# A retention and SwiGLU kernel on one core: the loads of the first four pairs, VectorE copies for the first pair, and sums and loads moved at the second token tile

## The chip, the core and the metric

The kernel runs on one core of a Trainium2 chip. The time is device microseconds of one launch. In these pages PE is TensorE (matmuls; PEld is its weight load), DVE is VectorE, ACT is ScalarE, POOL is GpSimd and SP is SyncE, which here only starts transfers. Each engine takes its own instructions in order and waits, where it must, for another engine or for a transfer (DMA). ACT and POOL can start transfers too. In such a queue a transfer is asked for when the engine arrives at the instruction.

## What is computed

```python
# q, k, v: (batch 8, heads 8, seq 576, head_dim 64), fp32
scores = scale * q @ k.T                       # scale = 1/sqrt(64)
gamma  = 1 - 2 ** (-5 - arange(heads))
rel    = pos[:, None] - pos[None, :]
D      = where(rel >= 0, gamma ** rel, 0)      # per head
att    = (scores * D) @ v
x      = att.transpose(0, 2, 1, 3).reshape(4608, 512)
g      = x @ w_gate                            # w_gate, w_val: (512, 1536)
y      = (g * sigmoid(g)) * (x @ w_val) @ w_out    # w_out: (1536, 512)
```

## The kernel before

**Attention.** The 64 heads are taken in 32 pairs `i`, four (`HP`) to a batch, a pair filling the 128 partitions. Retention is computed in chunks with a running state. `load(i)` (from L258) starts the transfers of a pair: the query and key in the layout for transposing (`qk`), the key (`kn`), the value (`v`) and the last rows of the value (`vl`, one transfer a head). `tick(t)` (L573) is one step of a pipeline three pairs deep. On PE it issues the own-chunk values of pair t-2, the state products of t-1, the earlier-chunk values of t-2 and the scores of t-1. What the other engines do for it stands in a list of pieces: first a copy of the even states (`even`) of t-1 together with the scaling of `kn` of pair t (`keys`), then the outputs of t-2 (`to_x`), the masks of t-1 (`own`, `states`), and the transposes of pair t into `qT` and `kT`, at last a load to come. `go_on(k)` (L595) issues the next k pieces, and the steps of the second half call it between their own instructions: once in an up step, three times in a down step, four times in `down0`.

For the first four pairs PE transposes query and key into three PSUM banks and ACT copies them out (L417, L420); from pair 4 on DVE transposes 32x32 blocks. `keys` run on ACT (L438), for pairs 10 to 12 on DVE (L435, by `vector(i)`). For pairs 12 to 19 (`light(i)`) ACT copies the outputs, and for the others DVE scales them.

**Weights.** They arrive as 64-bit numbers. `load_w(m)` (L343) starts the transfer of one block (1 MB) on ACT's queue, `split(j)` (L361) takes half a block apart on ACT, `rounding(j)` (L376) puts the fp32 value together on DVE. `load_w(0)`, `(1)` and `(2)` are called by `keys` of pairs 0, 1 and 2; every later one by the split that frees the place it goes to.

**The feed-forward part.** Its first token tile has 512 tokens and is done plainly: `up0(f)` (matmul L612) and `down0(f)` (L622) over 12 blocks of 128 hidden columns. The other four tiles have 1024 tokens each and go by a table of fast matrix multiplication (`UP`, `DOWN`): 26 up steps (L842) for each third (`qd`) of the hidden columns, and then 26 down steps (L881), each a product of a sum of input blocks with a sum of weight blocks. The sums of `w_out` (`out_sums`, POOL) are formed at the end of the first tile and stored in DRAM (`dn_ops`), on SP's queue, or on ACT's where a group is `late`. The sums of `w_gate` and `w_val` (`first_sums`, `w_sums`, issued by L648 through `add` and by L812) are formed in the up steps of the second tile on POOL, DVE and ACT, and stored (`up_ops`). Later tiles, and the down steps of the second one, fetch both through a ring of eight places (L739, SP), eight operands ahead.

Steps write into one of four PSUM banks. DVE reads a bank (L783, L786), ACT applies SiLU (L857), and DVE or POOL multiplies (L860, L864) into `hid`.

**Order.** The order on PE, DVE, ACT, POOL and SP is the order of the source from L906 on: ticks 0 to 5 with the first splits and roundings (from L908), then a list `plan` for `up0`, then the loop over `down0`, then the loop over the four large tiles (from L974). What stands before L906, such as the calls `load(0)` to `load(3)`, the identity matrix and the masks `near`, is put in order by the compiler's planner. Pairs 6 and on are loaded two pairs ahead by `next_load` (12 and 13 by `load` in the second tile's first up steps); the load of pair 10 is called in the plan's last but one block, that of pair 11 after the first `down0`. In the second tile (`n == 1`) ticks 12 to 17 lie in its up steps and 18 to 21 in its down steps, spaced out evenly by `merge` (L900): the latter come before down steps 0, 6, 13 and 19.

`first_sums(0)` is called in the `down0` loop, and `first_sums(qd + 1)` in up step 22 of the first two thirds of the second tile: four sums for the next third's first step (one each by ACT and DVE, two by POOL), then those of its second step, all ahead of that step's own bank reads in the queues.

Of the kernel before, what the change touches and what calls it, by code (L numbers as in the profile page):

```python
# [154 lines left out]
def kernel(  # L155
# [32 lines left out]
    nc = tc.nc  # L188
# [69 lines left out]
    def load(i):  # L258
# [6 lines left out]

        queues = (nc.sync, nc.scalar if i < 2 else nc.sync)

# [23 lines left out]
        for dst, src in ((kn, k), (t, v)):  # L291
            for hl in range(2):
                chunks(dst, src, hl)
        for hl in range(2):
            queues[hl].dma_start(out=last[half[hl]], in_=v[b, 2 * p + hl, CW:S, :])
        loaded[i] = (qk, kn, t, last)
# [10 lines left out]
    nc.sync.dma_start(out=tab[:, NCOL:], in_=decays[:, NCOL:])  # L307
    load(2)
    load(3)
    ident = const.tile([P, P], F32, name="ident")  # L310
# [9 lines left out]
    for hl in range(2):  # L320
        nc.gpsimd.affine_select(out=near[half[hl]], in_=inv[half[hl]].unsqueeze(2).to_broadcast([L, H, L]),
                                compare_op=ALU.is_ge, fill=0.0, base=0, pattern=[[0, H], [1, L]], channel_multiplier=-1)
        nc.gpsimd.tensor_copy(out=last_near[half[hl]], in_=near[half[hl], hl::2])


# [76 lines left out]
    def vector(i):  # L402

        return 10 <= i <= needed(1) - 2

    def transposes(i):
        p = i % HP
        qk, kn, vt, last = loaded.pop(i)
        qT = qp.tile([P, S], F32, tag="qT", name="qT")
        st[i] = dict(qT=qT, kn=kn, v=vt, last=last)  # L410
        pieces = []
        if i < HP:

            for t, src, bank in ((qT, qk[0], bankA), (kT, kn, bankB)):
                for c in range(NFULL):
                    nc.tensor.transpose(bank[:, ts(c, P)], src[:, c].rearrange("p h d -> p (h d)"), ident)
                nc.scalar.copy(out=t[:, 0:CW], in_=bank)  # L417
            nc.tensor.transpose(bankC[:, 0:P], qk[1].rearrange("p h d -> p (h d)"), ident)
            for n, t in enumerate((qT, kT)):
                nc.scalar.copy(out=t[:, CW:S], in_=bankC[:, n * L : (n + 1) * L])  # L420
        else:
            if light(i):
                def scale_q():

                    src = qk[:, 0].rearrange("p (j r) d -> p r j d", r=2)
                    for r in range(2):
                        nc.scalar.activation(out=src[:, r], in_=src[:, r], func=AF.Copy, scale=piece[:, 2 * p + r : 2 * p + r + 1])
                pieces.append(scale_q)
            for n, t in enumerate((qT, kT)):
                pieces.append(lambda n=n, t=t: nc.vector.transpose(out=t, in_=qk[:, n].rearrange("p j d -> p (j d)")))  # L430

        def keys():
            for hl in range(2):
                if vector(i):
                    nc.vector.tensor_scalar(out=kn[:, :, hl, :], in0=kn[:, :, hl, :],  # L435
                                            scalar1=key[:, 2 * p + hl : 2 * p + hl + 1], scalar2=None, op0=ALU.mult)
                else:
                    nc.scalar.activation(out=kn[:, :, hl, :], in_=kn[:, :, hl, :], func=AF.Copy,  # L438
                                         scale=key[:, 2 * p + hl : 2 * p + hl + 1])
            if i < RAWS:  # L440
                load_w(i)

        if light(i):
            return [lambda: (keys(), pieces[0]())] + pieces[1:]
        return [keys] + pieces
# [127 lines left out]
    def tick(t, lo=HP, hi=NP, spread=False, then=None):  # L573
# [10 lines left out]
        keys, *new = transposes(t) if lo <= t < hi else (lambda: None,)  # L584
        pieces.append(lambda: (copies(), keys()))
        if lo <= t - 2 < hi:
            pieces.extend(to_x(t - 2))
        pieces.extend(masks)
# [226 lines left out]

    def first_sums(qd):

        engines = [nc.scalar, nc.gpsimd, nc.vector, nc.gpsimd]
        for op, eng in zip(up[0][5], engines, strict=True):
            if op[0] == "neg":  # L820
                nc.scalar.mul(out=up_view(qd)(int(op[1])), in_=up_view(qd)(int(op[2])), mul=-1.0)
            else:
                add(eng, op, up_view(qd))
        w_sums(qd, 1)

    def up_step(n, qd, i):
# [17 lines left out]
        if busy:  # L844
            nc.scalar.dma_start(out=up_ops[qd][i].rearrange("p (g x) -> p g x", g=2), in_=w)
            if i == 22 and qd + 1 < NQ:
                first_sums(qd + 1)
            if qd + 1 == NQ and i >= 22:
# [90 lines left out]
    for f in range(2, NF):  # L939
# [4 lines left out]
        if f in tick_at:  # L944
            plan.append(lambda t=tick_at[f]: tick(t, HP, FIRST))
        if f == NF - 2:
            plan.append(lambda t=tick_at[f]: next_load(t))
# [10 lines left out]
    for m, f in enumerate(down_order):  # L958
        down0(f)
        if m == 0:  # L960
            next_load(9)
        go_on(4)
# [3 lines left out]
        if m == 8:  # L966
            first_sums(0)
        if m > 8:
# [12 lines left out]
    for n in range(1, NTILE):  # L981
# [3 lines left out]
        if n == 1:  # L985

            for i in range(N):
                ups.pop(0)()
                if i in (6, 14):
                    load(FIRST + i // 14)  # L990
        for a, b, steps in ((done, cut, ups), (cut, upto, [lambda i=i: down_step(n, i) for i in range(N)])):
            merge((0.0, ticks(a, b)), (0.5, steps))
        done = upto
# [30 lines left out]
```

## Time and profile before

| | |
|---|---|
| median of 6 runs | 1082.82 us (1080.19 to 1087.33) |
| the profiled execution | 1082.78 us, of which the span 1081.1 us |
| mean granted clock of TensorE | 0.991 |
| PE busy | 1041.9 us (96%) |
| DVE busy | 645.4 us (60%) |
| POOL busy | 401.7 us (37%) |
| ACT busy | 275.8 us (26%) |
| weight loads of PE (beside its matmuls) | 857.4 us (79%) |
| DMA, mean rate | 184 GB/s |

The profile cuts the span into 40 equal slices and gives each engine a digit for each slice, its busy share in tenths; PEclk is the clock that the throttle granted to TensorE in tenths of full speed. A group of instructions is shown as line, engine, operation, output and inputs with their shapes and the number of instructions, then its busy time and the mean of one in ns (or start and length in us where single instructions are listed), and in brackets the engine's idle time just before and what ended it. SPq is SP's queue, ACTq ScalarE's. A sum of busy times says little of the end: PE has 96% of the span, so what matters is where PE stands still and what ends each pause.

### The profile page before, as it was taken

The page shows a single profiled execution, that of the slowest core. Times are in us where ns is not written, and L with a number is a line of the kernel's source. Part 1 is how long each engine was busy: PE and PEld are TensorE (multiplying, and loading weights), DVE is VectorE, ACT ScalarE, POOL GpSimd, SP SyncE. Part 2 cuts the span into 40 slices and gives each one's busy share as a digit, 9 for nine tenths or more (in the row PEclk, how much of TensorE's full clock was granted, in tenths as well). Part 3 has the DMA queues.
Part 4 walks back from the last instruction along what each step waited for, and adds up shares of the span by engine and source line. Part 5 has one row for each costly group of instructions (what it writes and reads, how often), then busy time and mean ns, then how long its engine had stood idle before and what let it go on. Part 6 is the DMA issues. An engine that isn't in the chain of part 4 may idle for free.

```text
span 1081.1 us, 21477 instructions
## 1 busy us (share of the span) xinstructions
PE 1041.9 (96%) x8420; PEld 857.4 (79%) x8420; DVE 645.4 (60%) x1063; ACT 275.8 (26%) x588; POOL 401.7 (37%) x357
## 2 busy tenths in 40 slices
PE   5999995999999899999999999999999999999998
PEld 4545553688878788888888888888888888888887
DVE  1577743876877866754646868535267465244644
ACT  3465500223343211223232111122221012231110
POOL 1002369475455402741215025622151375122505
PEclk9899997999999999999999999999999999999999
DMA  9979766665567788767567778554565555555653
GB/s 226 236 227 250 212 177 197 190 193 173 167 177 197 234 192 246 207 178 199 147 171 213 180 188 248 155 150 137 154 174 152 161 177 154 152 151 158 182 167 98
DMA packets 304212, 198.58 MB, mean 184 GB/s; under 512 B 219632, under 2 KB 247280, under 8 KB 304112
## 3 DMA queue, kind: packets, MB, share of 16 engines
q1 hardware_dynamic: 272512, 152.80, 53.5%
q10 hardware_dynamic: 31600, 44.41, 12.2%
q8 instruction: 67, 1.10, 0.4%
q14 instruction: 33, 0.27, 0.1%
HBM read 157.04 MB, written 40.11 MB: 182 GB/s over the span
## 4 chain that ended last, share of the span: by engine, by line
PE 84%; DVE 6%; POOL 3%; issue 2%; DMA 2%; SPq 2%; ACT 1%; ACTq 0%; DVEq 0%; POOLq 0%
PE bankE L842 11%; PE bankA L842 11%; PE bankC L842 11%; PE bankB L842 11%; PE bankE L881 6%; PE bankB L881 6%; PE bankC L881 6%; PE bankA L881 6%; PE outer L482 2%; PE bankA L612 2%; PE bankC L612 2%; PE bankB L612 2%; DVE rest L783 2%; PE bankE L612 2%; PE outer L459 2%
## 5 line engine op out<-in xcount | busy, mean ns | idle before, releaser
L783 POOL TENSOR_TENSOR rest<-rest 128x512 f32<-128x512 f32 x56 | 79.1, 1418 | 297.4 <-DVE rest L783 279.0
L857 ACT ACTIVATE io<-rest 128x256 f32<-128x256 f32 x180 | 75.0, 417 | 347.1 <-DVE rest L783 301.3
L842 PE MATMUL bankC<-rest,arena 128*128 128x256 f32 x544 | 129.3, 381 | 1.5 <-DVE rest L783 1.4
L842 PE MATMUL bankA<-rest,arena 128*128 128x256 f32 x544 | 129.0, 380 | 1.3 <-DVE rest L783 1.3
L648 POOL TENSOR_TENSOR arena<-arena 128x512 f32<-128x512 f32 (+1 forms) x72 | 114.7, 1606 | 34.9 <-DMA up<-arena 25.2
L648 POOL TENSOR_TENSOR rest<-rest 128x256 f32<-128x256 f32 (+1 forms) x86 | 79.5, 944 | 126.0 <-DVE rest L384 88.9
L842 PE MATMUL bankB<-rest,arena 128*128 128x256 f32 x512 | 121.5, 380 | 1.2 <-DVE arena L860 0.8
L842 PE MATMUL bankE<-rest,arena 128*128 128x256 f32 x512 | 121.5, 380 | 0.2 <-DVE rest L783 0.2
L842 PEld LDWEIGHTS bankA<-rest,arena 128*128 128x128 f32 x544 | 103.1, 190 | 16.7 <-issue 2.1
L842 PEld LDWEIGHTS bankC<-rest,arena 128*128 128x128 f32 x544 | 102.8, 190 | 16.7 <-issue 2.6
L864 POOL TENSOR_TENSOR arena<-rest,io 128x256 f32<-128x256 f32 x72 | 51.9, 727 | 167.1 <-ACT io L857 167.1
L842 PEld LDWEIGHTS bankB<-rest,arena 128*128 128x128 f32 x512 | 97.0, 190 | 15.3 <-DVE arena L860 1.2
L842 PEld LDWEIGHTS bankE<-rest,arena 128*128 128x128 f32 x512 | 97.0, 190 | 13.9 <-issue 0.6
L783 DVE TENSOR_TENSOR rest<-bankB,rest 128x512 f32<-128x512 f32 x72 | 48.9, 687 | 64.7 <-PE bankB L842 46.7
L783 DVE TENSOR_TENSOR rest<-bankC,rest 128x512 f32<-128x512 f32 x72 | 49.0, 688 | 64.0 <-PE bankC L842 43.9
L783 DVE TENSOR_TENSOR rest<-bankE,rest 128x512 f32<-128x512 f32 x72 | 48.8, 686 | 63.7 <-PE bankE L842 45.5
L783 DVE TENSOR_TENSOR rest<-bankA,rest 128x512 f32<-128x512 f32 x72 | 48.8, 686 | 63.0 <-PE bankA L842 45.7
L860 DVE SCALAR_TENSOR_TENSOR arena<-rest,io 128x256 f32<-128x256 f32 x84 | 55.6, 666 | 12.3 <-ACT io L857 12.3
L881 PE MATMUL bankB<-arena 128*128 128x256 f32 x252 | 58.3, 381 | 0.0
L881 PE MATMUL bankA<-arena 128*128 128x256 f32 x252 | 58.1, 381 | 0.0
L881 PE MATMUL bankC<-arena 128*128 128x256 f32 x252 | 58.0, 380 | 0.0
L881 PE MATMUL bankE<-arena 128*128 128x256 f32 x252 | 57.9, 380 | 0.0
(155 smaller groups left out, 1627.2 us busy)
## 6 DMA issues: line engine op xcount, KB each, us to landing
arena<-up SPq DMA_DIRECT2D x234, 256.0 KB, 2.6
arena<-dn SPq DMA_DIRECT2D x104, 384.0 KB, 3.5
up<-arena ACTq DMA_DIRECT2D x78, 256.0 KB, 2.7
out_dram<-rest SPq DMA_DIRECT2D x32, 256.0 KB, 3.5
qk<-in_q_dram SPq DMA_DIRECT2D x112, 72.0 KB, 2.9
qk<-in_k_dram SPq DMA_DIRECT2D x112, 72.0 KB, 2.6
v<-in_v_dram SPq DMA_DIRECT2D x62, 128.0 KB, 2.9
kn<-in_k_dram SPq DMA_DIRECT2D x58, 128.0 KB, 3.0
```

Source lines behind the costliest of these rows:

```text
L459: m = nc.tensor.matmul(xo[half[hl ^ r * exchange(i)], c, r], s["v"][half[r], c, hl, :], ret[half[r], hl, c], start=(c == 0), stop=(c == 0) ...
L482: nc.tensor.matmul(xr[half[hl]] if c + 1 == NC else xo[half[hl ^ c % 2 * exchange(i)], c // 2, c % 2], state[half[hl], c, :], s["qT"][half ...
L612: nc.tensor.matmul(bank, w_up[:, f // 4, gv, f % 4, c // 2, (c % 2) * P : (c % 2 + 1) * P], xs[0][:, c, :], start=(c == 0), stop=(c == HP ...
L648: eng.tensor_tensor(out=dst, in0=srcs[0], in1=srcs[1], op=ALU.add if op[0] == "add" else ALU.subtract)
L783: eng.tensor_tensor(out=at(op[1]), in0=at(op[2]), in1=at(op[3]), op=ALU.add if op[0] == "add" else ALU.subtract)
L842: nc.tensor.matmul(b[:, gv * TB : (gv + 1) * TB], w[:, gv, ts(c, P)], rhs[:, c, :], start=(opens and gv == 0 and c == 0), stop=(c == 1), s ...
L857: nc.scalar.activation(out=s, in_=src[:, 0:TB], func=AF.Silu, scale=-1.0 if negative else 1.0)
L860: return lambda: nc.vector.scalar_tensor_tensor(out=dst, in0=src[:, TB : 2 * TB], scalar=-1.0, in1=s, op0=ALU.mult, op1=ALU.mult)
L864: nc.gpsimd.tensor_tensor(out=dst, in0=src[:, TB : 2 * TB], in1=s, op=ALU.mult)
L881: nc.tensor.matmul(b[:, m * TB : (m + 1) * TB], lhs[:, qd, ts(m, P)], w[:, qd], start=(opens and qd == 0 and m == 0), stop=(qd == NQ - 1), ...
```

## The change

Seven edits, of which the first three concern the start:

1. In `load`, the second head's transfers of pairs 2 and 3 are issued by POOL; before, by SP. `load(2)` and `load(3)` stand behind the identity matrix and the masks in the source.
2. The last rows of the value are one transfer for both heads from pair 4 on; before, two.
3. Pair 0's copies out of PSUM and its key scaling are on DVE; before, on ACT. `load_w(0)`, `(1)` and `(2)` are called by `keys` of pairs 1, 2 and 3.
4. In a tick whose outputs ACT copies (pairs 12 to 19), the outputs ride with the first piece; before, they were a piece of their own. Every later piece of such a tick is issued one `go_on` earlier.
5. `first_sums` of thirds 1 and 2 is issued in two parts: two sums at up step 22, the other two and the second step's sums at step 25.
6. The load of pair 11 is called in the plan, ahead of the last block's `out_sums` groups; before, after the first `down0`.
7. In the second tile, ticks 18 to 21 come before down steps 2, 7, 13 and 19.

```diff
@@ load
-        queues = (nc.sync, nc.scalar if i < 2 else nc.sync)
+        queues = (nc.sync, nc.scalar if i < 2 else nc.gpsimd if i < HP else nc.sync)
...
-        for hl in range(2):
-            queues[hl].dma_start(out=last[half[hl]], in_=v[b, 2 * p + hl, CW:S, :])
+        if i < HP:
+            for hl in range(2):
+                queues[hl].dma_start(out=last[half[hl]], in_=v[b, 2 * p + hl, CW:S, :])
+        else:
+            nc.sync.dma_start(out=last, in_=v[b, 2 * p : 2 * p + 2, CW:S, :])
...
     load(0)
     load(1)
     nc.sync.dma_start(out=tab[:, NCOL:], in_=decays[:, NCOL:])
-    load(2)
-    load(3)
     ident = const.tile([P, P], F32, name="ident")
     make_identity(nc, ident)
...
         nc.gpsimd.tensor_copy(out=last_near[half[hl]], in_=near[half[hl], hl::2])
+
+    load(2)
+    load(3)
...
     def vector(i):
-        return 10 <= i <= needed(1) - 2
+        return i == 0 or 10 <= i <= needed(1) - 2
@@ transposes
+        copy = nc.scalar.copy if i else nc.vector.tensor_copy
...
-                nc.scalar.copy(out=t[:, 0:CW], in_=bank)
+                copy(t[:, 0:CW], bank)
...
-                nc.scalar.copy(out=t[:, CW:S], in_=bankC[:, n * L : (n + 1) * L])
+                copy(t[:, CW:S], bankC[:, n * L : (n + 1) * L])
...
-            if i < RAWS:
-                load_w(i)
+            if 0 < i <= RAWS:
+                load_w(i - 1)
@@ tick
-        pieces.append(lambda: (copies(), keys()))
-        if lo <= t - 2 < hi:
-            pieces.extend(to_x(t - 2))
+        outputs = to_x(t - 2)[0] if lo <= t - 2 < hi else lambda: None
+        if t - 2 >= 0 and light(t - 2):
+            pieces.append(lambda: (copies(), keys(), outputs()))
+        else:
+            pieces.extend([lambda: (copies(), keys()), outputs])
@@ first_sums
-    def first_sums(qd):
+    def first_sums(qd, lo, hi):
         engines = [nc.scalar, nc.gpsimd, nc.vector, nc.gpsimd]
-        for op, eng in zip(up[0][5], engines, strict=True):
+        for op, eng in list(zip(up[0][5], engines, strict=True))[lo:hi]:
...
-        w_sums(qd, 1)
+        if hi == 4:
+            w_sums(qd, 1)
@@ up_step
-            if i == 22 and qd + 1 < NQ:
-                first_sums(qd + 1)
+            if i in (22, 25) and qd + 1 < NQ:
+                first_sums(qd + 1, *((0, 2) if i == 22 else (2, 4)))
@@ plan
-        if f == NF - 2:
+        if f >= NF - 2:
             plan.append(lambda t=tick_at[f]: next_load(t))
@@ down0 loop
         down0(f)
-        if m == 0:
-            next_load(9)
         go_on(4)
...
-            first_sums(0)
+            first_sums(0, 0, 4)
@@ large tiles
-        for a, b, steps in ((done, cut, ups), (cut, upto, [lambda i=i: down_step(n, i) for i in range(N)])):
-            merge((0.0, ticks(a, b)), (0.5, steps))
+        downs = [lambda i=i: down_step(n, i) for i in range(N)]
+        merge((0.0, ticks(done, cut)), (0.5, ups))
+        if n == 1:
+            for i, f in reversed(list(zip((2, 7, 13, 19), ticks(cut, upto), strict=True))):
+                downs.insert(i, f)
+            merge((0.5, downs))
+        else:
+            merge((0.0, ticks(cut, upto)), (0.5, downs))
```

## The prediction

> **What bounds the kernel now.** I read the page's slices first: a slice is 27 us, and TensorE (PE) is short of work in the first slice (digit 5), in the seventh (5) and a little in the tenth to fourteenth (8s and 9s).
>
> ```profile
> PE   5999995999999899999999999999999999999998
> POOL 1002369475455402741215025622151375122505
> PEclk9899997999999999999999999999999999999999
> ```
>
> The busy time by stages puts numbers on it (the two figures after each stretch are its length and PE's busy time; the PE clock stands before the last two).
>
> ```profile
> 0.00:38.00 38.00, 23.57 (x513) 21.33 (x513) 13.56 (x37) 15.43 (x37) 2.88 (x11) 0.91 0.93 233
> 38.00:165.00 127.00, 126.82 (x1200) 64.90 (x1199) 79.00 (x165) 53.01 (x95) 34.33 (x46) 1.00 0.80 217
> 165.00:184.00 19.00, 6.96 (x140) 5.55 (x139) 6.88 (x19) 1.15 (x2) 18.43 (x26) 0.64 0.70 205
> ...
> 249.50:306.70 57.20, 53.30 (x548) 45.45 (x548) 45.80 (x69) 20.96 (x48) 31.16 (x24) 1.00 0.59 170
> 306.70:372.30 65.60, 62.48 (x659) 53.86 (x653) 51.20 (x81) 26.42 (x64) 35.53 (x24) 1.00 0.78 207
> ```
>
> PE idles 14.4 us before 38, 12.0 in 165 to 184, 3.9 and 3.1 in the second tile's gate/value products, next to nothing elsewhere. Only these places can pay; 38 to 165 and all after 372.3 are PE work, where an edit can at best do no harm. So next I read the chain of waits through the first 38 us, then who ended each PE gap.
>
> **Start: the first pair on VectorE (DVE).** In the chain, start, length and what:
>
> ```profile
> 7.83 1.28 ACT L417
> 9.12 0.59 ACT qT L417
> ...
> 10.43 0.41 ACT kn L438
> 10.89 1.42 PE inner L468 x29
> ```
>
> ScalarE issues its ten loads until 7.80, loads a table (1.28), then copies, so PE gets kn at 10.84 although PE's transposes into bankA, bankB and bankC ended at 4.8, 6.8 and 7.1. On DVE, idle until 16.66: two 128x512 PSUM copies by the row of L630 (0.69 each), two 64-column copies (0.21, row L510), one L435 scaling before PE can start (0.35). kT starts at 6.84: 7.5, 7.9, 8.2. PE starts new_states(0) at about 8.2 instead of 10.89: 2.65 us. From there to 38 the chain is PE, ACT, DVE in turn, about 8.1 us a tick, with no DMA in it, so 2.65 would be carried through if nothing asked for later becomes late.
>
> **Weights one pair later.** load_w(1) is issued on ACT after keys(2) instead of keys(1): 25.97 in the trace, 23.3 with the shift, against 19.56. Behind it ACT does split(0), split(1), then split(2), which reads it, and behind split(2) on the same engine stand pair 3's copies, on the chain at 31.25. Two L370/L371 passes cost 1.25. Landing of a 1 MB weight: 5.7 us in the stretch before 26, median 7.2 and 6.3 (two each) in 15 to 40; alone, at the 390 GB/s of 21 to 24, 2.7 plus about 2.2 of latency = 4.9 (estimate from those rows). I take 5.3, as four pair loads are asked for earlier now. It lands at 28.6, split(2) ends 29.85, pair 3 starts 1.4 us earlier than now instead of 2.65: **gain 1.3**. Bounds: 2.65 if it lands by 27.3; minus 1 if it takes 7.7. load_w(0) moves to about 14.7 and has 8.7 us until split(0); load_w(2) delays split(4) to about 38, now 37.94: no cost.
>
> **GpSimd (POOL) as third queue.** No row shows a POOL-issued DMA. POOL is idle from 5.0 to 121; ten issues at SP's 0.51 to 0.6 take 6, at 1 us each 10 (guess at twice SP's price). Pair 2 is needed at 19.9, pair 3 at 28.0: nothing either way. The Trainium skill (SBUF — State Buffer, "SBUF: two separate sides") says a DVE operation in a two-port mode locks POOL out while it writes descriptors, and speaks against this: pair 0's two SBUF scalings are 0.35 each, so 0.7 of a slack of over 4; also nothing.
>
> **load(11) issued earlier in the source.** This gap is the largest prize:
>
> ```profile
> 177.72 1.14 PE L459 MATMUL outer<-ret,v 64*64 64x64 f32 x32 [11.68 <-DVE ret_last L510]
> 174.57 0.35 DVE L435 TENSOR_SCALAR kn<-kn,tab 128x256 f32<-128x256 f32 x1 [18.53 <-DMA kn<-in_k_dram]
> SPq L288 <- DMA dn<-rest: 15.4, 6, 3.6
> ```
>
> DVE's keys(11) wait for kn, and SP cannot issue it, since six of its eight query/key DMAs wait for earlier dn stores (third line: SP waits, total, times). In the compiled program of before, SP and ACT share eight completion semaphores in turn, each DMA waits for its predecessor on the same one, and the turns follow the planner's clock: between load(11)'s DMAs stand three or four ACT stores each. Those stores are paced by POOL's sums (18.43 of 19 us busy). The source order between two engines isn't used, and SP's own order is unchanged: f = 11's stores and those of m = 0 are late ones, on ACT. So I cost the move at **nothing** and leave the gap. Bound on the other side: all 11.7 plus 2.9 of slow matmuls afterwards (clock 0.64; the tick takes 5.5 instead of 2.6), but POOL's first sums end at 196.1 and PE's fourth step needs them at 203.06 + 3 x 1.73 = 208.2: at most 12.1.
>
> **One DMA for both halves of vl.** 28 pairs save one SP issue of 0.51. It matters where SP's queue gates something: load(10) stands ahead of the dn stores that let POOL start at 151.53, so minus 0.55 there. Against it speaks a rule of the Trainium skill (DMA: Bandwidth & Descriptors, "Why a DMA increments its semaphore by 16 and not by 1"): the engines used are the largest number up to 16 that divides both patterns' slowest dimension. That is now 64 on each side; the merged source has 2 heads outermost, so 2 engines with 64 rows each. By the row, SP's queue spends 34 ns a packet (53.5% of 16 x 1081 us over 272512): 60 more in a line cost 2.0 us for whatever follows on those engines. By the rule POOL's third store lands about 1.3 later, net +0.75; by today's vl row alone (2.2 us to landing), -0.55. Between them, **+0.2**. Elsewhere the ring is eight fetches ahead of PE.
>
> **Second tile.** The first sums are split between steps 22 and 25. Now DVE waits in line for POOL twice:
>
> ```profile
> 246.97 1.74 DVE L648 TENSOR_TENSOR arena<-arena 128x512 f32<-128x512 f32 x1 [2.41 <-POOL arena L812]
> 300.11 1.74 DVE L648 TENSOR_TENSOR arena<-arena 128x512 f32<-128x512 f32 x1 [1.72 <-POOL arena L812]
> 252.20 1.99 PE L842 MATMUL bankB<-rest,arena 128*128 128x256 f32 x8 [0.77 <-DVE arena L860]
> 305.98 0.27 PE L489 MATMUL outer<-qT,kT 64*64 64x64 f32 x2 [1.71 <-DVE kT L430]
> 372.27 2.83 PE L881 MATMUL bankB<-arena,rest 128*128 128x256 f32 x12 [1.88 <-DMA arena<-dn]
> ```
>
> Behind the waiting sum stand the bank reads that PE needs. Three steps later the POOL product is long done; the moved POOL sums fall into 251.5 to 256.57, idle now, and are needed at 255.8. So 0.77 goes. A light tick's output copies ride with keys, so each later piece runs a step (1.73) earlier: kT is before tick 15, and 1.71 goes; but states (1.85 of DVE) now come ahead of step 20's bank read, whose reader PE waits 0.4 us later by my order of the DVE rows: 1.3 net. At the end of this tile, load(19) is asked for 4 us earlier (kT at 356.6, not 360.5), so the 1.88 wait for dn goes; but tick 18 no longer covers the last products: hid slot 1 is ready at 361.2, PE would start the first down step at 360.1, and the same DVE reordering costs 0.6 before it: 0.5 net. **Gain 2.6**, bounds 0 and 5.5 (all of the named gaps plus the 0.9 at 297.85).
>
> **Sum.** 1.3 + 2.6 - 0.2 = 3.7. The profiled execution took 1082.78 (span 1081.1, 1.7 around it), and the median of the runs is 1082.82, so there is no offset: **1079.1**.
>
> **Rivals.** *The kn gap closes* (0.15): the planner's turns come out with load(11) ahead of the stores. For it: the moved line is where that load is asked for; against it: the three-to-four interleave holds through all 24 stores alike. 12.1 more: 1067; halved, 1073. *Weights too late* (0.22), the slower side: an ACT issue of a weight blocks on its semaphore's predecessor as at 37.46 and 43.87 (2.7 and 3.4 us after ACT was free). If that hits load_w(1) and load_w(2), w1 lands at 23.3 + 3.2 + 6.6 = 33.1, pair 3 starts 3.1 late, and even(3) behind split(4) makes PE's tick 5 wait 4 more: +7.1 - 2.6 + 0.2 = 1087.5. It decides once w1 lands after 30.0. *Nothing arrives* (0.08): DVE's order in the second tile eats its gain and w1 lands at 30: 1082.8. The forecast has 0.55.
>
> **Numbers.** 0.3% (3.2 us) is about what tells a change from none here. Forecast's own range 1076 to 1082; with the rivals 1069 to 1087. Faster by over 0.3% (under 1079.6): 0.7 of the forecast and the closed gap, 0.54; slower 0.22; the rest within.
>
> **What would show it.** Right: PE's L468 near 8.2; pair 3's first qT copy near 29.9; DVE's kn gap near 172 still 17 to 19 us with SP waiting for dn stores; no DVE L648 wait for L812; no wait for arena<-dn at the first down steps. Wrong: that kn gap under 10 us (the gap rival), or ACT idle before split(2) past 30 (the weights rival); a vl landing over 4 us shows the two-engine rule.

## The result: 0.9971 of before, from other places than forecast

The changed kernel takes 1080.13 us (median of 32 runs), the kernel before 1083.75 (69 runs). The ratio is 0.9971, 95% interval 0.996 to 0.9982: 3.1 us less, between 1.9 and 4.3. In a later group of runs the same kernel stood at 0.9984 (0.9965 to 1.0003). The forecast was 3.7 us less. Its total was right; two of its three main terms were not.

The profiled execution of the changed kernel spans 1076.6 us, before 1081.1: this pair lies 4.5 apart, more than the runs do, so its differences are read for their places first. Where they arise is seen from the starts of a few PE instructions, in us of the span:

| | before | changed | moved in this stretch |
|---|---|---|---|
| first product of up0 | 37.95 | 38.14 | +0.2 |
| first product after the pause near 166 | 177.72 | 175.50 | -2.4 |
| first up product of the second tile | 203.1 | 200.9 | +0.1 |
| last down product (bank E) | 1076.8 | 1071.9 | -2.7 |

So the start gave nothing, the pause got shorter by 2.4 though it was forecast to stay, and the second tile gave what was forecast. The busy times by stage of the changed kernel say the same (length, then PE, PEld, DVE, ACT and POOL with their instruction counts, the granted PE clock, the DMA share, GB/s).

```profile
0.00:38.00 38.00, 23.41 (x512) 21.23 (x512) 15.89 (x43) 13.22 (x30) 9.96 (x21) 0.91 0.95 238
38.00:165.00 127.00, 126.82 (x1210) 65.02 (x1203) 78.52 (x165) 53.16 (x95) 35.48 (x48) 1.00 0.78 218
165.00:184.00 19.00, 8.98 (x145) 6.30 (x144) 9.23 (x25) 1.15 (x2) 18.43 (x26) 0.73 0.69 202
...
249.50:306.70 57.20, 56.10 (x563) 48.07 (x562) 42.83 (x66) 23.19 (x55) 31.42 (x24) 1.00 0.69 186
306.70:372.30 65.60, 63.78 (x660) 54.72 (x659) 53.10 (x79) 22.77 (x55) 34.55 (x23) 1.00 0.77 216
```

PE is as busy as before in the first 38 us (23.41 against 23.57), 2 us busier in 165 to 184, and 2.8 and 1.3 us busier in the two stretches of the second tile.

**The start.** The chain of waits of the changed kernel (start, length, what):

```profile
8.70 1.27 PE inner L475 x29
...
17.91 6.39 DMA qk<-in_q_dram
24.30 0.02 issue
24.32 5.59 DMA rest<-in_moe_w_val_dram
...
30.00 0.66 ACT rest L374
30.66 0.55 ACT rest L375
31.21 0.47 ACT qT L423
```

PE does get the first pair early, at 8.70 instead of 10.89. But the chain then leaves PE: a query transfer of pair 4 lands at 24.3, only then does ScalarE get to ask for weight 1 (24.32; its keys had ended at 23.48), that lands 5.6 us later, and split(2) and pair 3's first copy follow at 30.00 and 31.2. Before, pair 3's first copy was at 31.25. The head start of 2.2 us ends there.

**The pause.** VectorE's wait for kn in the changed kernel, and PE's behind it:

```profile
172.69 0.38 DVE L441 TENSOR_SCALAR kn<-kn,tab 128x256 f32<-128x256 f32 x1 [16.46 <-DMA kn<-in_k_dram]
...
175.50 1.14 PE L466 MATMUL outer<-ret,v 64*64 64x64 f32 x32 [9.26 <-DVE ret_last L517]
```

The same wait, 2.4 us shorter. SP's own waits are the same too (total, times, longest): six of load(11)'s transfers stand behind dn stores for 15.5 us, 15.4 before.

```profile
SPq L288 <- DMA dn<-rest: 15.5, 6, 6.0
```

What moved is when SP arrives there. Its queue before and then in the changed kernel (start and length of the issues; vl is the last transfer of a load, the dn stores stand behind it):

```profile
111.89 1.11 SPq L295 DMA_DIRECT2D vl<-in_v_dram  x2
113.10 11.40 SPq L699 DMA_DIRECT2D dn<-rest  x9
...
132.28 1.11 SPq L295 DMA_DIRECT2D vl<-in_v_dram  x2
133.49 6.51 SPq L699 DMA_DIRECT2D dn<-rest  x9
...
147.80 1.11 SPq L295 DMA_DIRECT2D vl<-in_v_dram  x2
149.01 3.96 SPq L699 DMA_DIRECT2D dn<-rest  x8
```

```profile
111.71 0.55 SPq L298 DMA_DIRECT2D vl<-in_v_dram  x1
112.36 11.37 SPq L708 DMA_DIRECT2D dn<-rest  x9
...
131.18 0.54 SPq L298 DMA_DIRECT2D vl<-in_v_dram  x1
131.82 6.65 SPq L708 DMA_DIRECT2D dn<-rest  x9
...
145.12 0.54 SPq L298 DMA_DIRECT2D vl<-in_v_dram  x1
145.76 4.88 SPq L708 DMA_DIRECT2D dn<-rest  x8
```

The stores come 0.74, 1.67 and 3.25 us earlier. Each spared vl issue (0.56) stays spared for what follows in the same queue, so it adds up over the loads of pairs 8, 9 and 10. (In the last step there is chance too: before, one kn issue of load(10) took 1.2 us longer.) The other profiles agree. Counted from each kernel's own first up0 product, the first store behind these three loads is asked for 75.4, 96.4 and 111.3 us later on the mean of the three kernels below with two vl transfers (before, vl_undone, tile2_alone), and 74.3, 94.1 and 108.2 us later on the mean of the eight with one in which ScalarE asks for the weights: 1.1, 2.2 and 3.1 us earlier, and at none of the three stores do the two groups overlap. That is about 1 us a load, more than one issue; what gives the rest is not shown.

Not all of this lead arrives. POOL's third batch of sums starts at 149.77 instead of 151.53, 1.8 earlier and not 3.25, and kn of pair 11 is asked for at 169.34 instead of 171.53. The reason stands under *vl in one transfer* below.

**The second tile.** PE's pauses of the changed kernel there:

```profile
292.37 1.99 PE L852 MATMUL bankB<-x_odd,arena 128*128 128x256 f32 x8 [0.76 <-DVE rest L792]
...
348.34 2.00 PE L852 MATMUL bankB<-x_odd,arena 128*128 128x256 f32 x8 [0.76 <-DVE rest L792]
...
365.74 2.83 PE L891 MATMUL bankB<-arena,rest 128*128 128x256 f32 x12 [0.48 <-DMA arena<-dn]
...
390.95 2.86 PE L891 MATMUL bankA<-arena 128*128 128x256 f32 x12 [1.33 <-DVE arena L657]
```

The 0.77 for hid and the 1.71 for kT are gone, the wait for dn is 0.48 instead of 1.88, and VectorE no longer waits for a sum of GpSimd there. New are two waits of 0.76 for a bank read of VectorE, and 1.33 for a sum of hid on VectorE.

### The profile page after: what moved, and what is told of

It reads as the page before. It is cut to its first block, busy times and chain, and to the rows that moved or that the text cites. A ratio compares the mean times of both kernels' runs of the same rounds, so it can differ in the third digit from the quotient of the medians.

```text
span 1076.6 us, 21471 instructions
## 1 busy us (share of the span) xinstructions
PE 1041.6 (97%) x8420; PEld 857.1 (80%) x8420; DVE 648.8 (60%) x1069; ACT 273.2 (25%) x582; POOL 408.5 (38%) x367
## 4 chain that ended last, share of the span: by engine, by line
PE 84%; DVE 5%; DMA 3%; POOL 3%; issue 2%; SPq 2%; ACT 1%; ACTq 0%; DVEq 0%; POOLq 0%
PE bankC L852 11%; PE bankE L852 11%; PE bankB L852 11%; PE bankA L852 11%; PE bankA L891 6%; PE bankB L891 6%; PE bankC L891 6%; PE bankE L891 6%; DVE rest L792 2%; PE bankA L621 2%; PE outer L489 2%; PE bankC L621 2%; PE bankB L621 2%; PE bankE L621 2%; PE outer L466 2%
## 5 line engine op out<-in xcount | busy, mean ns | idle before, releaser
L852 PEld LDWEIGHTS bankC<-rest,arena 128*128 128x128 f32 x544 | 102.9, 190 | 15.4 <-issue 1.2
```

The source lines that it names most:

```text
L852: nc.tensor.matmul(b[:, gv * TB : (gv + 1) * TB], w[:, gv, ts(c, P)], rhs[:, c, :], start=(opens and gv == 0 and c == 0), stop=(c == 1), s ...
```

## The experiments

Twelve more runs, one of them of the changed kernel again, each beside the kernel before. Four figures are read from each one's profiled execution. *up0* is the start of the first up0 product. *First stage* runs from there to the second tile's first up product, and holds the pause. *Rest* runs from there to the last down product. *Pauses* is the sum of PE's pauses between 235 and 400 us that the list of PE's rows shows.

| kernel | ratio to before (interval) | up0 | first stage | rest | pauses |
|---|---|---|---|---|---|
| before | | 37.95 | 165.1 | 873.7 | 7.6 |
| changed | 0.9971 (0.9960 to 0.9982) | 38.14 | 162.8 | 871.0 | 4.8 |
| after_again | 0.9984 (0.9965 to 1.0003) | 38.15 | 163.7 | 873.2 | 7.0 |
| vl_alone | 0.9977 (0.9961 to 0.9992) | 37.67 | 165.8 | 874.6 | 8.5 |
| vl_undone | 1.0001 (0.9985 to 1.0018) | 40.72 | 166.3 | 871.7 | 5.4 |
| start_undone | 0.9956 (0.9940 to 0.9972) | 40.07 | 164.5 | 872.7 | 6.5 |
| weights_as_before | 0.9963 (0.9946 to 0.9980) | 41.55 | 163.8 | 871.5 | 5.3 |
| weights_by_pool | 0.9946 (0.9922 to 0.9970) | 35.35 | 164.8 | 871.2 | 5.0 |
| tile2_alone | 0.9995 (0.9977 to 1.0013) | 38.13 | 166.5 | 872.9 | 6.6 |
| pieces_undone | 0.9957 (0.9935 to 0.9978) | 36.26 | 162.1 | 870.3 | 5.0 |
| downs_undone | 0.9961 (0.9943 to 0.9980) | 39.02 | 166.1 | 870.6 | 4.6 |
| key11_first | 0.9946 (0.9929 to 0.9963) | 39.25 | 159.3 | 873.7 | 5.7 |
| key_value11_pool | 0.9931 (0.9906 to 0.9957) | 34.27 | 160.6 | 875.0 | 5.7 |
| split_alone_best | 0.9916 (0.9885 to 0.9946) | 36.30 | 159.9 | 873.2 | 4.6 |

A profile is one execution, and the same program differs from one to the next by 1 to 3 us in up0 and first stage: up to the second tile *changed*, *after_again*, *pieces_undone* and *downs_undone* are the same program, and so are *vl_alone* and *start_undone*. So means are read where there are several. In the expectations the pause is placed "before tick 11"; on PE it lies before the products of tick 12, which wait for what tick 11 gave VectorE.

**vl in one transfer, alone and taken back.** The edit is this, made in the kernel before and taken out of the changed one:

```diff
-        for hl in range(2):
-            queues[hl].dma_start(out=last[half[hl]], in_=v[b, 2 * p + hl, CW:S, :])
+        if i < HP:
+            for hl in range(2):
+                queues[hl].dma_start(out=last[half[hl]], in_=v[b, 2 * p + hl, CW:S, :])
+        else:
+            nc.sync.dma_start(out=last, in_=v[b, 2 * p : 2 * p + 2, CW:S, :])
```

vl_alone:

> The kernel before with one edit: vl of both heads in one transfer from pair 4 on. Theory (SP's queue carries load after load, so each spared issue before the pause adds up): VectorE's pause before keys(11) ends about 2.2 us earlier, PE's 11.7 us pause becomes about 9.4, the first up product of the second tile starts near 200.8 instead of 203.1, and the time falls by about 2.3 us (0.2%). Rival (the move of load(11) or the new start shortened the pause): the pause stays within 0.6 us of 11.7 and the time within 0.1%. Second rival (one transfer of two outer rows is carried by two engines): vl takes over 4 us to land.

vl_undone:

> The changed kernel with vl again in two transfers. Theory (vl alone shortened the pause): PE's pause before tick 11 is back at 11.2 to 12.2 us and the time is about 2.3 us above the changed kernel's, near 0.999 of before. Rival (another part shortened it): the pause stays near 9.3.

The times answer both ways: alone the edit gives 0.9977, which is 2.5 us (0.9 to 4.2), and without it the changed kernel is at 1.0001 (0.9985 to 1.0018), clear of the changed kernel's first interval, though not of that of after_again. In vl_undone's own group it is also 3.5 and 4.3 us slower on the mean than weights_as_before and start_undone, which have the one transfer and differ from it otherwise only in the start. So the edit gains; about 2.5 us is the best figure, and each of the figures is uncertain by over 1 us.

The single profile of vl_alone didn't show what was expected: its pause is 11.39 us. A v issue of its load(10) took 2.34 us instead of 1.06, which ate part of the lead. downs_undone, with one vl transfer too, has 2.43 there and a pause of 11.06. Over the executions the first stage is 166.0 on the mean of the three kernels with two vl transfers (165.1, 166.3, 166.5), and 164.2 on the mean of the eight with one and pair 11's load in its old order (162.8, 163.7, 165.8, 164.5, 163.8, 164.8, 162.1, 166.1), though those two groups overlap. vl_undone's pause is 11.86 as expected. The move of load(11) isn't the cause: vl_undone has it, and with that one line at its old place the changed kernel compiles to the same program.

The two-engine rival holds, and it names the price of the edit. The traces keep the counts by which a transfer reports its end. Every other transfer of the SP and ScalarE queues reports 16; each of the 28 merged vl reports 3, one about 1 us after the issue and two as it lands, which fits two engines and not 16. It lands 3.3 us after its issue (median, *changed*), two separate ones after 2.3 (*before*); the expectation's sign, over 4 us, was set too high: load(10)'s vl landed after 3.0 to 3.2. What stands behind it is later too: the first dn store behind load(10) takes 3.5, 2.8 and 2.8 us to land (*changed*, *after_again*, *vl_alone*) against 1.9 (*before*, *tile2_alone*), and POOL's third batch starts 3.5 us after that store's issue on the mean of all eleven kernels with one vl transfer (3.2 to 4.0), against 2.5 in each of the three with two. So the merged transfer costs about 1.0 us there, and gains because the queue is 3.1 ahead.

**The start, taken back.** The changed kernel with queues, copies and weights of before:

```diff
-        queues = (nc.sync, nc.scalar if i < 2 else nc.gpsimd if i < HP else nc.sync)
+        queues = (nc.sync, nc.scalar if i < 2 else nc.sync)
...
-        return i == 0 or 10 <= i <= needed(1) - 2
+        return 10 <= i <= needed(1) - 2
...
-            if 0 < i <= RAWS:
-                load_w(i - 1)
+            if i < RAWS:
+                load_w(i)
```

> The changed kernel with its whole start as before: loads 2 and 3 on SP and at their old place, pair 0 on ScalarE, weights at pairs 0, 1 and 2. Theory (the start's three edits together bring nothing): the first up0 product starts at 38.0, and the time is within 0.1% of the changed kernel's. Rival (the start gained 1.3 us as forecast, and the one profiled execution hides it): this one is 1.3 us slower than the changed kernel.

It isn't slower (0.9956 against 0.9971, and 0.9984 for after_again). Its up0 starts at 40.07, not 38.0: the start varies by more than the edits are worth. The rival of a gain of 1.3 falls; whether the new start costs a little isn't settled, as the intervals overlap.

**The changed kernel again.**

> The changed kernel once more, for a second profiled execution beside the others of this group. Theory (the start brings nothing and varies by some us from execution to execution with the granted clock): the ratio to before is 0.996 to 0.998 again, the first up0 product starts anywhere from 38 to 41, and the start's pause of ScalarE before split(2) ends at weight 1's landing. Rival (the start gains 1.3 as forecast): the first up0 product starts at 36.7 or before.

Up0 at 38.15, and split(2) waits 3.77 us for weight 1:

```profile
22.45 0.37 ACTq L355 DMA_DIRECT2D rest<-in_moe_w_val_dram  x1
...
30.59 0.66 ACT L374 ACTIVATE rest<-rest 128x512 f32<-128x512 f32 x1 [3.77 <-DMA rest<-in_moe_w_val_dram]
```

Here the asking was not held up (22.45 against 24.32 in the first execution), and the landing took 8.05 us instead of 5.59. The two executions lose the head start in different ways and to the same end. Over the six executions with the new start, up0 begins at 38.6 on the mean (36.26 to 40.72), over the four with the old one at 38.5 (37.67 to 40.07). In all six new ones ScalarE waits 2.7 to 3.8 us for weight 1, and split(2) starts at 30.5 on the mean (28.65 to 32.41). The one with the earliest, pieces_undone at 28.65, has the earliest up0, 36.26.

**The weights at pairs 0 to 2 again**, with VectorE's copies and GpSimd's transfers kept:

```diff
-            if 0 < i <= RAWS:
-                load_w(i - 1)
+            if i < RAWS:
+                load_w(i)
```

> The changed kernel with the first three weights asked for at pairs 0, 1 and 2 again, while VectorE still copies pair 0 and GpSimd still asks for heads. Theory (the later weight 1 ate the head start): ScalarE no longer waits for weight 1 before pair 3's copies, the first up0 product on PE starts at 35.5 to 36.3 instead of 38.2, and the time falls by about 2 us against the changed kernel. Rival (the transfers of the first 38 us fill the engines, so weights asked for earlier only make pairs 2 and 3 late): the first up0 product starts at 37.5 or later.

The theory failed: up0 starts at 41.55. The rival's sign came out, but not its cause: PE transposes pair 3 at 26.90, earlier than in the changed kernel (28.03), so that pair wasn't late. ScalarE's rows in this kernel:

```profile
19.96 0.37 ACTq L355 DMA_DIRECT2D rest<-in_moe_w_val_dram  x1
...
27.66 0.37 ACTq L355 DMA_DIRECT2D rest<-in_moe_w_gate_dram  x1
28.08 0.66 ACT L374 ACTIVATE rest<-rest 128x512 f32<-128x512 f32 x1 [4.70 <-DMA qk<-in_q_dram]
...
33.55 0.37 ACTq L355 DMA_DIRECT2D rest<-in_moe_w_val_dram  x1
34.02 0.66 ACT L374 ACTIVATE rest<-rest 128x512 f32<-128x512 f32 x1 [3.60 <-DMA kn<-in_k_dram]
```

Weight 1 is asked for in time, at 19.96. But now the asking for the next two (27.66 and 33.55) holds ScalarE up for 4.7 and 3.6 us, each time behind a transfer of another pair, and split(0) and split(2) stand behind it in order. So it isn't only when a weight is asked for. ScalarE, asking while the loads' transfers are under way, waited here for one of theirs, and its arithmetic waited with it. This execution took 1083.15 us, 2.3 above this kernel's median, and the kernel's ratio, 0.9963, is no worse than the changed kernel's: 4.7 and 3.6 are what one execution shows, not a steady cost.

**The first two weights from GpSimd.** This takes ScalarE out of that:

```diff
-                nc.scalar.dma_start(out=dst[:, :, cols], in_=src[:, :, cols])
+                (nc.gpsimd if m < 2 else nc.scalar).dma_start(out=dst[:, :, cols], in_=src[:, :, cols])
```

> The changed kernel with the first two weights asked for by GpSimd instead of ScalarE. Theory (weight 1's late asking, and ScalarE's own queue held up at it, eat pair 0's head start): both are asked for at 11 to 15 us, ScalarE never waits for weight 1, the first up0 product starts 1.5 to 2.5 us earlier than in the changed kernel, and so does everything after. Rival (the transfers of the first 30 us fill the engines): pairs 2 and 3 land late in its place, and the first up0 product is no earlier.

GpSimd asks, and ScalarE's splits follow without a wait for a weight:

```profile
11.13 1.52 POOL L355 DMA_DIRECT2D rest<-in_moe_w_gate_dram  x2
12.65 0.75 POOL L355 DMA_DIRECT2D rest<-in_moe_w_val_dram  x1
```

```profile
26.18 0.68 ACT L374 ACTIVATE rest<-rest 128x512 f32<-128x512 f32 x1 [0.54 <-ACT rest L375]
26.76 0.67 ACT L375 ACTIVATE rest<-rest 128x512 int32<-128x512 uint32 x1
28.66 0.59 ACT L423 COPY qT<-bankA 128x512 f32<-128x512 f32 x1 [1.23 <-PE bankA L422]
```

Pair 3's first copy is at 28.66 and waits for PE, not for a weight. Up0 starts at 35.35: all of VectorE's head start arrives. The two later kernels with this edit have 34.27 and 36.30, so the mean of the three is 35.3, against 38.6 with the new start and 38.5 with the old one. The time is 0.9946, against 0.9984 for the changed kernel in the same group: 3.3 us less on the mean of 12 runs each, between 1.4 and 5.2. The later pause gives part back: kn of pair 11 is asked for at 168.01, only 1.3 us earlier than in the changed kernel.

**The second tile alone.** The kernel before with the split first sums, the outputs riding with the keys and the moved ticks (edits 4, 5 and 7 of the change):

> The kernel before with the second tile's three edits alone: the split first sums, the outputs riding with the keys, and ticks 18 to 21 at down steps 2, 7, 13 and 19. Theory: PE's pauses between the second tile's first product and its eighth down step fall from 6.4 to 7.4 us to between 3.6 and 5.4, and the time by about 2.6 us (0.2 to 0.3%). Rival (VectorE's new order eats it): pauses stay above 6 us and the time within 0.1%.

By its time (0.9995) this can't be told from no change, and its pauses are 6.6, above the range expected, so that by its two signs the rival came out in this run. The pauses hang on one of them: the wait before the fourth down product is 2.61 here. That wait varies within one program: 0.48 in the one execution of the changed kernel and 2.66 in the other. Over the seven executions with all three edits and an otherwise unchanged pause, *rest* is 872.0 on the mean, against 874.2 for the two without them. That is 2.1 us by the profiles. By the times there is a second comparison: start_undone is vl_alone with these three edits (and the moved load(11), which changes nothing), both with 22 runs in one group, and it is 1.8 us faster on the mean (0.4 to 3.1). So the second tile gains about 2 us; tile2_alone's own interval allows up to 2.5.

**Outputs as a piece of their own again:**

```diff
-        outputs = to_x(t - 2)[0] if lo <= t - 2 < hi else lambda: None
-        if t - 2 >= 0 and light(t - 2):
-            pieces.append(lambda: (copies(), keys(), outputs()))
-        else:
-            pieces.extend([lambda: (copies(), keys()), outputs])
+        pieces.append(lambda: (copies(), keys()))
+        if lo <= t - 2 < hi:
+            pieces.extend(to_x(t - 2))
```

> The changed kernel with the outputs of pairs 12 to 19 as a piece of their own again. Theory: the wait for kT at the tick near 300 (1.4 to 1.7 us before) comes back, the two waits of 0.76 for a VectorE read that the shift made go, two of 0.9 come back in their place, and the time is about 1.3 us above the changed kernel's. Rival (the split first sums alone removed the kT wait): no wait for kT there.

PE's pauses there:

```profile
290.95 1.97 PE L850 MATMUL bankA<-rest,arena 128*128 128x256 f32 x8 [0.42 <-DVE rest L790]
...
346.61 1.97 PE L850 MATMUL bankC<-rest,arena 128*128 128x256 f32 x8 [0.91 <-DVE rest L790]
...
364.15 2.83 PE L889 MATMUL bankB<-arena,rest 128*128 128x256 f32 x12 [2.47 <-DMA arena<-dn]
```

No wait for kT. The rival holds: the split sums had taken it away. The shift of the pieces only traded 0.42 and 0.91 for twice 0.76 and, in the changed kernel, 0.26.

**Ticks 18 to 21 at down steps 0, 6, 13 and 19 again:**

```diff
-            for i, f in reversed(list(zip((2, 7, 13, 19), ticks(cut, upto), strict=True))):
-                downs.insert(i, f)
-            merge((0.5, downs))
+            merge((0.0, ticks(cut, upto)), (0.5, downs))
```

> The changed kernel with ticks 18 to 21 again at down steps 0, 6, 13 and 19. Theory (the new places trade one wait for another): the pause of 1.33 us before a down step that waits for VectorE's sum of hid near 391 goes, and the pause at the third or fourth down step, 0.5 to 2.7 in the changed kernel, is 1.9 to 2.9; sum of the second tile's pauses within 1 us of the changed kernel's. Rival (the new places are worth 0.5 us or more by themselves): the pauses sum to over 1 us more.

As the theory had it: the 1.33 is gone, and the wait before the fourth down product is 1.90. The pauses sum to 4.6, no more than in the changed kernel (4.8 and 7.0). Over all profiles, the wait at the first down products is 1.6 on the mean of the ten kernels with the moved ticks and 2.2 on the mean of the four without (before, vl_alone, this one and split_alone_best): the move saves 0.6 there and adds 1.33 later, in nine of the ten (not in pieces_undone).

**kn of pair 11 ahead of its query and key:**

```diff
+            if i == 11:
+                for hl in range(2):
+                    chunks(kn, k, hl)
             for n, src in enumerate((q, k)):
...
-        for dst, src in ((kn, k), (t, v)):
+        for dst, src in ((t, v),) if i == 11 else ((kn, k), (t, v)):
```

> The changed kernel with pair 11's kn asked for ahead of its eight query and key transfers. Theory (the pause before tick 11 is kn's place in SP's queue behind transfers that wait for dn stores, not the amount of data): kn is asked for by 156, VectorE's keys(11) come before 162, PE's pause before tick 11 is under 2 us, the tick takes 2.6 us at full clock, and the time falls by 9 to 12 us against the changed kernel (0.985 to 0.989 of before). Rival (PE waits next for kT of pair 11, or for POOL's late sums at the second tile's fourth step): half of that, 4 to 6 us. Second rival (kn's own place is not free before tick 10's products): no change.

SP's queue in this kernel, and PE's pause:

```profile
150.92 0.98 SPq L269 DMA_DIRECT2D kn<-in_k_dram  x2
152.01 9.72 SPq L291 DMA_DIRECT2D qk<-in_q_dram  x4
164.47 5.62 SPq L291 DMA_DIRECT2D qk<-in_k_dram  x4
170.47 2.19 SPq L269 DMA_DIRECT2D v<-in_v_dram  x2
```

```profile
173.71 0.45 PE L478 MATMUL inner<-v,kn 64*64 64x64 f32 x2 [5.73 <-DMA v<-in_v_dram]
```

kn comes 18 us earlier and the old pause is gone, but PE now waits 5.73 (and then 0.78) for v of the same pair, which still stands behind the eight transfers. So 6.5 us of pauses stand where 10.0 stood (9.26 and 0.76), and two short waits appear in the second tile, 0.70 for a sum of GpSimd and 0.57 for a bank read of VectorE. The gain against the changed kernel in the same group, 3.3 us on the mean (2.1 to 4.6), is a little under the first rival's range, and most of what is left of the pause waits for v, which neither side named.

**kn and v ahead, and the weights from GpSimd:**

```diff
+            if i == 11:
+                for dst, src in ((kn, k), (t, v)):
+                    for hl in range(2):
+                        chunks(dst, src, hl)
...
-        for dst, src in ((kn, k), (t, v)):
+        for dst, src in () if i == 11 else ((kn, k), (t, v)):
...
-                nc.scalar.dma_start(out=dst[:, :, cols], in_=src[:, :, cols])
+                (nc.gpsimd if m < 2 else nc.scalar).dma_start(out=dst[:, :, cols], in_=src[:, :, cols])
```

> The changed kernel with the first two weights asked for by GpSimd, and with pair 11's kn and v both asked for ahead of its query and key. Theory (the two effects are in different places; the pause before tick 11 is a queue, and only v kept key11_first from the rest): PE's pauses at tick 11 come to under 2 us together, the second tile's first product starts at 190 to 194, and the time is 0.988 to 0.991 of before. Rival (GpSimd's last sums and the first sums of the second tile become the bound): a pause of 3 us or more for GpSimd appears in the second tile's first ten up steps, and the time stays at 0.991 to 0.994.

PE's pauses:

```profile
171.91 0.37 PE L500 MATMUL outer<-qT,kT 64*64 64x64 f32 x2 [5.52 <-DVE kT L440]
...
209.86 1.99 PE L856 MATMUL bankB<-rest,arena 128*128 128x256 f32 x8 [1.05 <-POOL arena L825]
212.42 1.99 PE L856 MATMUL bankE<-rest,arena 128*128 128x256 f32 x8 [0.57 <-DVE rest L796]
215.39 1.99 PE L856 MATMUL bankC<-rest,arena 128*128 128x256 f32 x8 [0.98 <-POOL arena L825]
```

The wait has gone on to the last of the pair's data, the key that becomes kT, and 2.6 us of waits follow, 2.0 of them for sums of GpSimd that are now late. The first up product is at 194.8. Neither side of the expectation holds in full: the pause is 5.5, not under 2, and the time, 0.9931, lies with the rival. Its interval lies below those of the kernel before and of the changed one.

**The same with the split sums alone in the second tile** (the two edits above taken back):

> key_value11_pool with two of the second tile's three edits taken back: outputs of pairs 12 to 19 as a piece of their own, and ticks 18 to 21 at down steps 0, 6, 13 and 19; of the three only the split first sums are left. Theory (the split alone carries what the second tile gains): no wait for kT near 300, no wait of 0.77 for hid near 250, no wait of 1.33 for VectorE's hid sum near 389; from 230 to 400 the pauses sum to 3.5 to 5.5 us, and the time stays within 0.15% of key_value11_pool (0.9915 to 0.9945 of before). Rival (the shifted outputs or the moved ticks are needed once the other is gone): a wait for kT of 1.4 us or more comes back near 300 and the pauses sum to 6 us or more.

No wait for kT near 300, none for hid near 250, none of 1.33; pauses 4.6, time 0.9916 (0.9885 to 0.9946), the lowest ratio of all; key_value11_pool's interval overlaps it. By these waits the split carries the second tile's gain, and the other two edits aren't needed for it.

## Why the prediction came out right, and where it did not

- **Start, forecast 1.3, found 0.** VectorE takes pair 0 nearly as costed: PE at 8.70, forecast 8.2. The term that failed is weight 1's landing, "It lands at 28.6": asked for at 23.3, landed 5.3 us later. In the first execution ScalarE asked at 24.32, as its issue waited for pair 4's query transfer, and the landing took 5.59; in the second it asked in time, at 22.45, and the landing took 8.05. split(2) started at 30.00 and 30.59, and at 30.5 on the mean of six executions: 1.9 late, more than the whole 1.3. (The 390 GB/s behind the forecast's 4.9 us is the rate of 22 to 24; 21 to 24 as a whole has 326, which makes it 5.4.) The rival "weights too late" named the held-up asking and put it too high (7.1 us). weights_by_pool shows that this is where the head start goes: with the asking on another engine, up0 starts 2.6 us earlier than before the change, where the forecast had 2.65 as its upper bound.
- **GpSimd's queue, forecast nothing.** Its ten issues take 0.54 to 0.97 us, within the bounds taken, and end at 11.1. Those beside VectorE's work on pair 0 (4.98 to 8.9) take 0.55 to 0.79, so no lockout shows in them. One reading was off: before the change GpSimd is idle until 93.9, not until 121. Nothing hangs on it.
- **load(11), forecast nothing.** Right: the same program comes out.
- **One vl transfer, forecast -0.2, found a gain of about 2.5 by the times, 1.8 on the mean of the profiles.** This is the step that failed most. The term mis-sized is the lead of SP's queue: the forecast counted the spared issue only for load(10), 0.55, while the loads before it stand in the same queue. The store behind load(10) was asked for 3.25 us earlier in the first pair of profiles and 3.1 on the mean. The other half of the term was right: the two-engine rule holds, and it cost about 1.0 where the forecast had 1.3. POOL's third batch, 0.75 later by the rule in the forecast, started 1.76 earlier, 2.1 on the mean, which is the 3.1 less the 1.0. So the pause that the forecast left in place shortened, by a queue that came sooner and not by a changed order.
- **Second tile, forecast 2.6, found 2.7 in the first pair of profiles and 2.1 on the mean.** The size holds, the cause doesn't in part. The 0.77 went as forecast. The 1.71 for kT was credited to the shifted pieces; the split sums took it: before, VectorE's queue stood 1.72 us at its sum behind GpSimd just ahead of that tick. The shift brought only its price, 0.4 as forecast (0.76, 0.26 and 0.76 of waits for 0.42 and 0.91). The moved ticks were to gain 0.5: the 1.33 wasn't forecast, the wait at the first down products mostly stayed (1.6 for 2.2 on the mean), and they lose about 0.5.

Together: 0 instead of 1.3, +1.8 to +2.5 instead of -0.2, 2.1 instead of 2.6. That the total fell within the forecast's own range is luck: two errors of opposite sign.

## What to carry over

A queue that is in order adds up: an issue spared in each of several loads counted here for every load ahead of the gate (3.1 us), not once (0.55). What the merged transfer itself costs in landing (1.0) is to be set against that. Before a transfer is asked for later or earlier, look at which engine asks: ScalarE was held up by other transfers, and everything behind the asking waited, so VectorE's head start was worth nothing until the asking had moved to GpSimd, which had nothing else to do. And where a pause has several transfers behind it, taking the first to the front only shows the next one: kn, then v, then the key.

## What the runs showed of the hardware

- The granted PE clock in the first 38 us differs between executions of one program, 0.91 and 0.87 in two of the changed kernel. It can fall to about a half in and after a wait of PE: in weights_as_before it is 0.50 to 0.53 from 30 to 38 us, with PE busy for 0.4 of these 8, and still 0.50 in the 2 us after, with PE busy throughout. A late transfer there was paid for again in slower matmuls. The two lowest starts of up0 without weights from GpSimd (36.26 and 37.67) go with the highest clock (0.96); which is cause and which effect isn't shown.
- Weight 1, 1 MB, took 5.45 us to land at best in the changed kernel's start (pieces_undone), 8.05 in after_again, and 10.4 where GpSimd asked for it at 12.65. Asked for that early, the slow landing did no harm: split(2) needed it at 26.18.
- The merged vl, whose source has two heads outermost, reported 3 completion counts instead of 16. It landed in 3.3 us where two transfers of half the size took 2.3, and the stores behind it in the queue landed about 1 us later.
